# A decode block whose first two weight tensors are stored with wider rows in DRAM

## The chip, the cores and the metric

The kernel runs on one core of one Trainium2 chip. The core has a matrix engine (TensorE, PE in the profile), VectorE (DVE), ScalarE (ACT), GpSimd (POOL) and SyncE (SP), an on-chip memory of 128 partitions (SBUF), accumulators for matrix products (PSUM), and 16 DMA engines that move data between DRAM and SBUF. The metric is the device time of one execution in microseconds (us), as the median of several runs.

## What is computed

A transformer block for one new token of each of 4 sequences, with model width 512: a modulation from the condition `c`, attention of 32 query heads over the last 2048 positions of a cache with 8 key/value heads, and a gated feed-forward part. All tensors are float32.

```python
x = A_x                                            # 4 x 1 x 512
mod = (silu(c) @ w_mod).reshape(4, 6, 1, 512)
sa, ca, ga, sb, cb, gb = (mod[:, n] for n in range(6))
h = layernorm(x) * (1 + ca) + sa
q = (h @ wq), 32 heads of 128
p = softmax(q . k_cache[:, :, 6144:] * 128 ** -0.5)
x = x + ga * ((p . v_cache[:, :, 6144:]) @ wo)
h = layernorm(x) * (1 + cb) + sb
x = x + gb * ((silu(h @ w1) * (h @ w3)) @ w2)
```

## The kernel before, in words

The host (`_layout`, lines 493 to 523) rearranges every tensor so that the kernel can fetch it with few large transfers. Each tensor in DRAM has one row for each of the 128 partitions, and a load (`load`, lines 174 to 178) copies the rows of a tensor, or a range of their columns, to a range of columns of SBUF. Before the change a row is as long as its data, so that the rows of a tensor follow one another without a gap. `w_mod_a` has 4096 elements of the first third of `w_mod` and 32 elements of `x` and `c` in a row: 4128 elements, 16512 B. `wq` has 16144 elements, 64576 B. The other 240 columns of `wq` that would make it 16384 come as `guests`, in eight small loads of three rows each, 5760 B a row (lines 202 to 204).

SBUF holds a ring of three slots of 16384 elements for each partition (lines 162 and 163). `w_mod_a` goes to slot 0 (line 186), `wq` to slot 1 (line 188), and keys and values of group 0 to slot 2 (line 205). A group is one key/value head for all 4 sequences. There are eight groups; the first seven are `kv_in`, each 128 rows of 16384 elements (65536 B). After them come `wo_mod` (half of `wo` and the other two thirds of `w_mod`), `last_k_wo` and `last_v` (keys and values of group 7 and a quarter of `wo`), the rest of `wo`, and `w1`, `w3` and `w2` (lines 393 to 412). `w2` has rows of 28672 B and is fetched in four pieces of columns, 8, 3, 2 and 1 of its 14 blocks (`W2_CUTS`, line 16), that is 16384, 6144, 4096 and 2048 B of each row.

The order of the loads is the order of the program: all of them are issued by SP, except `wq`, which ACT issues on its own queue. SP waits before a load until the slot's former contents were used: the second `kv_in` (line 296) waits for the end of the modulation that reads `w_mod_a`, the third (line 329) for the last query product that reads `wq`, and every later one for the products of an earlier group.

The arithmetic goes as follows. After `w_mod_a` has landed, the condition is activated, `x` is transposed and normalised, and 32 products give shift and scale (`mod_columns`, line 292). Then the queries of all heads are computed from `wq` (lines 306 to 315) and transposed. Each group computes its scores, an exponential, the transposes of the probabilities and the weighted values (`group`, lines 350 to 388). After the last group follow the output projection, the second modulation and the feed-forward part.

A small planner, `Program` (lines 44 to 145), records each operation with the SBUF and PSUM ranges that it touches and adds the waits between engines. All recorded operations carry line 59 in the profile. Ranges in DRAM are not recorded.

Of the kernel before, what the change touches and what calls it, by code (L numbers as in the profile page):

```python
# [9 lines left out]
P = 128  # L10
# [6 lines left out]
GUESTS = 240  # L17
# [130 lines left out]
def block_kernel(nc, w_mod_a, wq, guests, kv_in, wo_mod, last_k_wo, last_v, wo, w1, w3, w2, out):  # L148
# [7 lines left out]
    def sb(name, *shape):  # L156
        return nc.alloc_sbuf_tensor(name, (P, *shape), F32).ap()
# [5 lines left out]
    slots = [ring[:, n * 2 * HALF : (n + 1) * 2 * HALF] for n in range(3)]  # L163
# [10 lines left out]
    def load(dst, src, cuts=(0, 1), queue="sync"):  # L174
        step = src.shape[1] // cuts[-1]
        for lo, hi in zip(cuts[:-1], cuts[1:]):
            do(queue, "dma_start", dst[:, lo * step : hi * step], src[:, lo * step : hi * step])
        return dst[:, : src.shape[1]]
# [4 lines left out]

    first = load(slots[0], w_mod_a)
    wma, xt_sb, ct_sb = first[:, :4096], first[:, 4096:4112], first[:, 4112:]
    wq_t = load(slots[1], wq, queue="scalar")
    do("scalar", "preload_act_table_set", "natural_log_exp_and_others")
    kv = [None] * G  # L190

# [53 lines left out]
    xc, sq, h = (sb(n, P) for n in ("xc", "sq", "h"))  # L245
    ss, ln, r0, ve, a, r = (sb(n, 1) for n in ("ss", "ln", "r0", "ve", "a", "r"))
# [246 lines left out]
def _layout(i):  # L493
    import numpy as np

    def a(t):
        return np.ascontiguousarray(t)

    k = i["A_k_cache"][:, :, SK - W :, :].reshape(B, G, NT, 512, DH)
    v = i["A_v_cache"][:, :, SK - W :, :].reshape(B, G, NT, NC, P, DH)  # L500
    wm = i["w_mod"].reshape(4, P, 6, 4, P)
    xc = np.concatenate([i[n].reshape(B, 4, P).transpose(2, 1, 0).reshape(P, 16) for n in ("A_x", "c")], 1)
    w2 = i["B_w2"].reshape(14, P, D)
    wq = a(i["A_wq"].reshape(4, P, G, 512).transpose(1, 2, 0, 3)).reshape(P, 16384)
    guests = np.zeros((2, 12, 6, GUESTS), np.float32)
    for n, (at, lo, hi) in enumerate(GUEST_AT):
        for m in range(2):
            guests[m, lo:hi, n] = wq[at + 32 * m + lo : at + 32 * m + hi, 16384 - GUESTS :]
    wo = a(i["A_wo"].reshape(2, 4, R, P, D).transpose(0, 3, 1, 2, 4)).reshape(2, P, 8192)
    kv = np.concatenate([k.transpose(1, 4, 2, 0, 3).reshape(G, P, 8192), v.transpose(1, 4, 2, 0, 3, 5).reshape(G, P, 8192)], 2)  # L510
    return {
        "w_mod_a": np.concatenate([a(wm[:, :, :2].transpose(1, 0, 3, 2, 4)).reshape(P, 4096), xc], 1),
        "wq": a(wq[:, : 16384 - GUESTS]),
        "guests": guests.reshape(24, 6 * GUESTS),
        "kv_in": kv[: G - 1],
        "wo_mod": np.concatenate([wo[0], a(wm[:, :, 2:].transpose(1, 0, 3, 2, 4)).reshape(P, 8192)], 1),
        "last_k_wo": np.concatenate([kv[G - 1, :, :8192], wo[1, :, :4096]], 1),
        "last_v": a(kv[G - 1, :, 8192:]),
        "wo": a(wo[1, :, 4096:]),
        "w1": a(i["B_w1"].reshape(4, P, FF).transpose(1, 0, 2)).reshape(P, 4 * FF),  # L520
        "w3": a(i["B_w3"].reshape(4, P, FF).transpose(1, 0, 2)).reshape(P, 4 * FF),
        "w2": a(np.stack([w2[4 * j + c] for c, j in CHUNKS], 1)).reshape(P, NF * D),
    }
# [15 lines left out]
```

## Time and profile before

| | us |
|---|---|
| median of 3 runs | 242.15 |
| lowest and highest | 242.04, 242.48 |
| span of the profiled execution, first to last instruction | 240.8 |
| PE busy | 148.7 (62%) |
| DVE busy | 56.3 (23%) |
| ACT busy | 24.1 (10%) |

The page gives the span of the profiled execution and no time of its own beside it; the median of the runs is 1.35 us longer than the span. The DMA engines read 101.22 MB from DRAM, 420 GB/s over the span. In the tables by slices the span is cut into 40 equal parts, and each digit is a busy share in tenths.

### The profile page before, as it was taken

Reading aid. Unit: us, or ns where it says so; the run is one execution under the profiler, and the core shown is the slowest. Engines: PE = TensorE matmul, PEld = TensorE weight load, DVE = VectorE, ACT = ScalarE, POOL = GpSimd, SP = SyncE. Lnnn points to the kernel's source line nnn. Section 1 sums busy time; section 2 is a strip of 40 time slices with the busy share of each in tenths; the row PEclk is TensorE's granted clock in tenths of the full one; section 3 lists DMA queues with packets and bytes.
Section 4 is the critical chain, followed back from the end, with each engine's and each line's share of the span. In section 5 each row is a group of like instructions: output and inputs, shape, how many; then the busy total and the mean of one; then the engine's idle time right before and its main releaser. Section 6 shows DMA issues by size and latency. Waiting matters only on the chain.

```text
span 240.8 us, 2502 instructions
## 1 busy us (share of the span) xinstructions
PE 148.7 (62%) x1113; PEld 54.2 (22%) x1113; DVE 56.3 (23%) x141; ACT 24.1 (10%) x36; POOL 4.5 (2%) x12
## 2 busy tenths in 40 slices
PE   0000169982984962944867576667399719965876
PEld 0000133322322212201312222221042202422333
DVE  5000231034152024123132133130313104113210
ACT  2000000003003003001100300300200001320100
POOL 7000000000000000000000000000000000000000
PEclk9999997997696798879797799795759968995899
DMA  8999999999999999999999999999999999999994
GB/s 305 434 444 455 424 425 446 416 446 414 457 395 468 403 459 414 449 425 446 425 446 427 435 435 435 435 427 446 425 446 425 411 419 430 386 444 443 401 413 162
DMA packets 2937, 101.39 MB, mean 421 GB/s; under 512 B 472, under 2 KB 472, under 8 KB 880
## 3 DMA queue, kind: packets, MB, share of 16 engines
q1 hardware_dynamic: 2784, 92.99, 89.8%
q10 hardware_dynamic: 144, 8.27, 8.0%
q8 instruction: 8, 0.13, 0.2%
q14 instruction: 1, 0.01, 0.0%
HBM read 101.22 MB, written 0.03 MB: 420 GB/s over the span
## 4 chain that ended last, share of the span: by engine, by line
DMA 60%; PE 31%; DVE 5%; ACT 3%; issue 1%; ACTq 0%
DMA ring<-kv_in 33%; DMA ring<-w 16%; PE s_ps L59 14%; DMA ring<-w_mod_a 11%; PE bank L59 9%; PE o_ps L59 6%; DVE nm L59 3%; ACT p_sb L59 3%; PE a_ps L59 1%; DVE mod_a L59 0%; ACT work L59 0%; DVE p_sb L59 0%; DVE e L59 0%; DVE h L59 0%; DVE sq L59 0%
## 5 line engine op out<-in xcount | busy, mean ns | idle before, releaser
L59 PE MATMUL s_ps<-ring,qT 128*32 128x512 f32 x256 | 36.5, 722 | 20.3 <-DMA ring<-kv_in 13.3
L59 PE MATMUL bank<-ident,p_sb 128*128 128x128 f32 (+1 forms) x136 | 27.7, 353 | 30.8 <-ACT p_sb L59 30.7
L59 PE MATMUL o_ps<-ring,pT 128*16 128x512 f32 x256 | 38.4, 707 | 0.1
L59 PEld LDWEIGHTS bank<-ident,p_sb 128*128 128x128 f32 (+1 forms) x136 | 19.8, 178 | 52.5 <-ACT p_sb L59 31.7
L59 ACT ACTIVATE p_sb<-s_ps,nm 128x2048 f32<-128x2048 f32 (+1 forms) x11 | 16.5, 1501 | 139.7 <-DVE oT L59 104.1
L59 DVE TENSOR_REDUCE nm<-s_ps 128x1 f32<-128x2048 f32 x7 | 16.0, 2292 | 32.5 <-PE s_ps L59 32.5
L59 DVE COPY pT<-bank 128x64 f32<-128x64 f32 x32 | 7.2, 225 | 57.0 <-PE bank L59 57.0
L59 PEld LDWEIGHTS s_ps<-ring,qT 128*32 128x32 f32 x256 | 8.7, 129 | 46.9 <-issue 20.1
L59 PE MATMUL bank<-ident,xs 128*128 128x128 f32 x1 | 0.5, 476 | 27.8 <-POOL xs L59 27.8
L59 PE MATMUL s_ps<-ring,h2T 128*32 128x512 f32 (+1 forms) x64 | 9.0, 657 | 2.3 <-DMA ring<-w 2.3
L59 PE MATMUL s_ps<-ring,hT 128*32 128x512 f32 (+1 forms) x64 | 9.4, 705 | 0.0
L59 PEld LDWEIGHTS o_ps<-ring,pT 128*16 128x16 f32 x256 | 5.4, 99 | 11.9 <-issue 9.0
L59 DVE SCALAR_TENSOR_TENSOR o_own<-o_ps,rl,own 128x512 f32<-128x512 f32 x7 | 5.3, 751 | 11.1 <-PE o_ps L59 11.1
L59 PE MATMUL a_ps<-ring,oT 128*4 128x512 f32 x64 | 7.4, 592 | 0.0
L59 DVE TENSOR_REDUCE o_sum<-o_own 128x128 f32<-128x512 f32 x7 | 7.2, 1034 | 0.2
L59 PE MATMUL bank<-ring,sc 128*32 128x256 f32 (+1 forms) x64 | 6.9, 587 | 0.0
L59 PEld LDWEIGHTS bank<-ident,xs 128*128 128x128 f32 x1 | 0.2, 183 | 27.8 <-POOL xs L59 27.8
L59 DVE TENSOR_SCALAR e<-e 128x16 f32<-128x16 f32 x1 | 0.2, 175 | 23.3 <-ACT e L59 23.3
L59 DVE COPY qT<-bank 128x64 f32<-128x64 f32 x8 | 2.2, 280 | 12.4 <-PE bank L59 12.0
L59 DVE TENSOR_REDUCE mx<-s_ps 128x1 f32<-128x512 f32 x4 | 2.8, 692 | 9.0 <-PE s_ps L59 9.0
L59 PEld LDWEIGHTS s_ps<-ring,h2T 128*32 128x32 f32 x64 | 2.6, 130 | 7.3 <-issue 4.4
L59 PE MATMUL s_ps<-ring,hidT 128*32 128x64 f32 (+1 forms) x112 | 3.6, 274 | 0.3 <-DVE hidT L59 0.3
(97 smaller groups left out, 63.7 us busy)
## 6 DMA issues: line engine op xcount, KB each, us to landing
ring<-wq ACTq DMA_DIRECT2D x1, 8072.0 KB, 26.9
ring<-w SPq DMA_DIRECT2D x2, 3584.0 KB, 37.9
ring<-last_k_wo SPq DMA_DIRECT2D x1, 6144.0 KB, 30.1
ring<-last_v SPq DMA_DIRECT2D x1, 4096.0 KB, 39.5
ring<-w_mod_a SPq DMA_DIRECT2D x1, 2064.0 KB, 26.7
ring<-wo SPq DMA_DIRECT2D x1, 2048.0 KB, 41.8
ring<-w SPq DMA_DIRECT2D x1, 2048.0 KB, 43.1
ring<-w SPq DMA_DIRECT2D x1, 768.0 KB, 44.5
```

The costliest lines, as they stand in the source:

```text
L59: op = Op(engine, lambda: getattr(getattr(self.nc, engine), method)(*args, **kw), [])
```

## The change

The host stores `w_mod_a` with rows of 5120 elements (20480 B) and `wq` with rows of 17408 elements (69632 B). The new function `spaced` puts zeros behind the data of each row. The kernel loads the same columns as before, from the same tensors, in the same order, to the same places. Only the distance from one row to the next in DRAM is another.

```diff
-    first = load(slots[0], w_mod_a)
+    first = load(slots[0], w_mod_a[:, :4128])
     wma, xt_sb, ct_sb = first[:, :4096], first[:, 4096:4112], first[:, 4112:]
-    wq_t = load(slots[1], wq, queue="scalar")
+    wq_t = load(slots[1], wq[:, : 16384 - GUESTS], queue="scalar")
...
+    def spaced(t, row):
+        return np.concatenate([t, np.zeros((P, row - t.shape[1]), np.float32)], 1)
+
...
-        "w_mod_a": np.concatenate([a(wm[:, :, :2].transpose(1, 0, 3, 2, 4)).reshape(P, 4096), xc], 1),
-        "wq": a(wq[:, : 16384 - GUESTS]),
+        "w_mod_a": spaced(np.concatenate([a(wm[:, :, :2].transpose(1, 0, 3, 2, 4)).reshape(P, 4096), xc], 1), 5120),
+        "wq": spaced(wq[:, : 16384 - GUESTS], 17408),
```

## Rows read from the trace of the kernel before

**Rows 1.** The page: span, busy time by engine, and the DMA lines in 40 slices.

```profile
span 240.8 us, 2502 instructions
...
PE 148.7 (62%) x1113; PEld 54.2 (22%) x1113; DVE 56.3 (23%) x141; ACT 24.1 (10%) x36; POOL 4.5 (2%) x12
...
DMA  8999999999999999999999999999999999999994
GB/s 305 434 444 455 424 425 446 416 446 414 457 395 468 403 459 414 449 425 446 425 446 427 435 435 435 435 427 446 425 446 425 411 419 430 386 444 443 401 413 162
```

**Rows 2.** Chain of waits, its load links and the last arithmetic: start, duration (us), what.

```profile
0.73 26.68 DMA ring<-w_mod_a
...
67.41 38.51 DMA ring<-kv_in
...
190.94 38.54 DMA ring<-w
229.48 0.04 issue
229.52 3.71 PE s_ps L59 x20
```

**Rows 3.** Timeline of PE, scores of four groups: start, duration, operation, idle before, releaser.

```profile
86.61 3.64 PE L59 MATMUL s_ps<-ring,qT 128*32 128x512 f32 x32 [2.39 <-DMA ring<-kv_in]
...
105.96 4.93 PE L59 MATMUL s_ps<-ring,qT 128*32 128x512 f32 x32 [3.44 <-DMA ring<-kv_in]
...
125.31 5.34 PE L59 MATMUL s_ps<-ring,qT 128*32 128x512 f32 x32 [2.19 <-DMA ring<-kv_in]
...
144.66 3.64 PE L59 MATMUL s_ps<-ring,qT 128*32 128x512 f32 x32 [1.80 <-DMA ring<-kv_in]
```

**Rows 4.** DMA issues (KB, us to landing), then the timeline of these issues.

```profile
ring<-wq ACTq DMA_DIRECT2D x1, 8072.0 KB, 26.9
ring<-w_mod_a SPq DMA_DIRECT2D x1, 2064.0 KB, 26.7
...
0.73 0.39 ACTq L59 DMA_DIRECT2D ring<-wq  x1
0.73 0.38 SPq L59 DMA_DIRECT2D ring<-w_mod_a  x1
8.95 0.42 SPq L59 DMA_DIRECT2D ring<-kv_in  x1
34.19 14.84 SPq L59 DMA_DIRECT2D ring<-kv_in  x2
```

**Rows 5.** Packets by size, and queues: packets, MB, share of 16 engines.

```profile
DMA packets 2937, 101.39 MB, mean 421 GB/s; under 512 B 472, under 2 KB 472, under 8 KB 880
...
q1 hardware_dynamic: 2784, 92.99, 89.8%
q10 hardware_dynamic: 144, 8.27, 8.0%
```

**Rows 6.** Windows: stretch, busy by engine, PEclk, DMA share, GB/s; two early, three of kv.

```profile
5.90:6.40 0.50, 0.00 (x0) 0.00 (x0) 0.00 (x0) 0.00 (x0) 0.00 (x0) 1.00 4.11 1778
8.90:9.40 0.50, 0.00 (x0) 0.00 (x0) 0.00 (x0) 0.00 (x0) 0.00 (x0) 1.00 4.12 1778
84.30:84.80 0.50, 0.00 (x0) 0.00 (x0) 0.50 (x1) 0.00 (x0) 0.00 (x0) 1.00 2.43 1049
103.70:104.20 0.50, 0.00 (x0) 0.00 (x0) 0.50 (x1) 0.00 (x0) 0.00 (x0) 1.00 2.12 918
144.00:144.50 0.50, 0.00 (x0) 0.00 (x0) 0.50 (x1) 0.00 (x0) 0.00 (x0) 1.00 1.82 786
```

**Rows 7.** Windows of the stretches in which wo, then the first piece of w2 loads.

```profile
208.00:210.00 2.00, 2.00 (x24) 0.59 (x20) 0.08 (x1) 0.00 (x0) 0.00 (x0) 1.00 0.98 418
...
230.00:232.00 2.00, 2.00 (x25) 0.66 (x20) 0.00 (x0) 0.00 (x0) 0.00 (x0) 1.00 0.98 418
```

**Rows 8.** Windows of the first microseconds, and of the rest of the first loads.

```profile
1.00:2.00 1.00, 0.00 (x0) 0.00 (x0) 0.94 (x4) 0.85 (x1) 0.83 (x2) 1.00 0.89 215
2.00:3.00 1.00, 0.00 (x0) 0.00 (x0) 0.97 (x9) 0.43 (x1) 1.00 (x1) 1.00 1.73 631
3.00:4.00 1.00, 0.00 (x0) 0.00 (x0) 0.99 (x9) 0.00 (x0) 1.00 (x4) 1.00 1.07 452
4.00:26.00 22.00, 0.00 (x0) 0.00 (x0) 0.39 (x2) 0.00 (x0) 1.02 (x2) 1.00 0.95 413
```

## The prediction

> **What bounds the kernel now.** I read the page's span and slices first [rows 1]. TensorE is busy 62% of the span, but the DMA line stands at 9 tenths or more in 38 of 40 slices; only the first and the last are lower. The reader is to see one stream of loads, about 101 MB, that never stops. The chain of waits says the same [rows 2]: its long links are loads (w_mod_a, kv_in, w), and after the last w (this is w3) 11.3 us of arithmetic follow, while the pieces of w2 come in. In the timeline of TensorE the scores of one group begin 19.35 us after those of the group before (86.61, 105.96, 125.31, 144.66), each time released by kv_in [rows 3]. One kv load is 128 x 65536 B = 8.389 MB, so it streams at 8.389 MB / 19.35 us = 433.5 GB/s.
>
> The two loads that change open this stream. Both are issued at 0.73 us, on two queues, and land 26.7 and 26.9 us later, side by side; kv_in is issued behind them at 8.95 us and waits in the queue [rows 4]. So the question is only whether the first 27 us of the stream get shorter or longer. If they do, does the end move as well? The next kv load was issued at 34.19 us and the one after it 14.8 us later at most, by 49.0 us [rows 4]. The first loads end at 27.6 us and a kv load takes 19.35 us, so kv[0] ends at about 47 us and kv[1] at about 66 us: each successor is in the queue 13 us or more before its turn. What the first loads win or lose therefore goes through to w3 and the end, one for one.
>
> **The change part by part.** Terms are made against the span of 240.8 us of the profiled execution. The page does not give the time of this execution itself; the median of the three runs is 242.15 us, and I carry the difference of 1.35 us unchanged as what lies around the span.
>
> *Bytes.* The slices in front of the two loads take only the 4128 and 16144 elements that were there before, so the copied bytes stay 2.114 + 8.266 = 10.380 MB. If the unused elements were read too, it would be 128 x (3968 + 5056) B = 1.155 MB more, 2.67 us at 432.6 GB/s; the destination has no place for them, so I take 0.
>
> *Packets.* wq is 144 packets on its queue: 128 of one row each, and 16 more, which I take as one for each of the 16 DMA engines [rows 5]. A source whose rows lie apart could be cut differently. The kernel already has such loads: w2 is fetched in column pieces, with rows of 16384, 6144, 4096 and 2048 B that stand 28672 B apart, and guests by every fourth row. Between 2 KB and 8 KB the page counts 880 - 472 = 408 packets [rows 5], exactly 3 x 128 + 24, one per row. So a row apart from its neighbour is still one packet: 0. Nor is there a new instruction or wait: one issue of 0.38 us on SP and one of 0.39 us on ACT stay [rows 4].
>
> *Steady rate.* In the windows the packets count in the stretch in which they begin, so a short stretch can have a share above 1; GB/s divided by share is the rate while an engine is busy. For wq and w_mod_a it is 1778/4.11 = 432.6 and 1778/4.12 = 431.6 GB/s [rows 6]. For kv, whose rows already start on multiples of 4096 B from each other, it is 431.7, 433.0 and 431.9 [rows 6]. So the odd rows of 16512 and 64576 B run as fast as the aligned ones; there is nothing left to win. The other side is bounded too: wo lies contiguous with rows of 16384 B, the first piece of w2 has the same rows 28672 B apart, an odd multiple of 4096 as in the change, and both show 418 GB/s at a share of 0.98 [rows 7]. So spacing costs nothing either. Bounds from the spread of these quotients: 0.3% of 24 us, 0.07 us to either side; I take 0.
>
> [...]
>
> *The start.* Here the rows do differ. From 1 to 4 us the shares are 0.89, 1.73 and 1.07, while the bytes at 432.6 GB/s would need 215/432.6 = 0.50, 1.46 and 1.04 [rows 8]. The first packets of the sixteen engines are thus slow by 0.39 + 0.27 + 0.03 = 0.69 us each on average, and after that the deficit is gone: 4 to 26 us show 413 GB/s at 0.95 [rows 8]. The first loads last 26.9 us for 10.380 MB / 432.6 = 24.0 us of transfer; 0.7 of the 2.9 us beside it is this. No row shows how much of it hangs on where the rows begin, and there is no second cold start in the trace to compare. Bounds: all of it goes (-0.69 us), or the same again is added (+0.69 us). The nearest row to no effect is the steady stretch, where layout makes no difference, so I take 0 and keep both ends for the range.
>
> *Sum:* 240.8 + 0 + 0 + 0 + 0 = 240.8 us of span, 242.15 us of time. What a measurement of this kernel can tell from no change is about 0.2%, 0.48 us.
>
> **Rivals.** *Forecast, nothing changes, 0.53.* The stream is bound by the engines' own pace and not by where it reads. It gives 242.15, with the spread of the runs shown (242.04 to 242.48).
>
> *The start becomes quicker, 0.27.* For it: the first packets are the only ones below the pace, and they read precisely the two tensors that are moved; 69632 = 17 x 4096 and 20480 = 5 x 4096 place the starts of the sixteen engines' rows differently over the memory. Against it: part of the 0.69 us must be the first access itself, which no layout takes away. All of it gone gives 241.46; the case decides from 0.48 of the 0.69 us on. [...]
>
> *The start becomes slower, 0.18.* Before, consecutive rows begin 128 B and 3136 B further round within 4096 B (16512 = 4 x 4096 + 128, 64576 = 15 x 4096 + 3136); afterwards all begin at the same place in it. If the sixteen first packets, which begin together, then run into each other at the memory, the deficit of 1 to 4 us doubles: 0.69 us more, 242.84. It decides from 0.48 us more. For it: sixteen starts inside about half a microsecond. Against it: kv rows begin in the same way and run at pace [rows 6], though no longer in step.
>
> *The change does something else than it says, 0.02.* The spaced rows are cut or read whole; the price of the second is 2.67 us, 244.8. The packet counts speak against it.
>
> **How the numbers follow.** The likeliest case gives 242.15. Its own range is 241.9 to 242.5: the steady bounds and the spread of the runs. The range over all cases reaches to where the two start rivals would end in full, 241.46 and 242.84: 241.4 to 242.8, leaving out effects beyond the bound and the last rival. Faster 0.27, within 0.2% 0.53, slower 0.18 + 0.02 = 0.20.
>
> **What would show it.** Right: the queue of wq has 144 packets and 8.27 MB; the rate while busy in short stretches before 26 us is 431 to 433 GB/s; the shares of 1 to 4 us still exceed need by 0.6 to 0.8 us; the scores of groups keep 19.35 us between them; w3 arrives within 0.3 us of 229.5. The faster case shows the excess below 0.2 us and w3 at about 228.8; the slower one an excess of about 1.4 us and w3 at about 230.2. The forecast is wrong if the steady quotient moves by a per cent, or if the end moves without the landing of the first loads having moved.

## The result, and the profile after

The changed kernel takes 242.66 us (median of 11 runs, 242.27 to 243.13) where the kernel before takes 242.15 (11 runs, 242.00 to 242.48): a ratio of 1.0018, 95% interval 1.0010 to 1.0026. It is slower by about half a microsecond. That lies inside the stated range, and just inside the 0.2% that the prediction had set as no change; but the interval excludes 1, and the forecast of no effect was wrong.

The page and the DMA view of the kernel after. They answer to [rows 1, 5]: the counts of packets and bytes are the same, the span is 0.5 us longer.

```profile
span 241.3 us, 2502 instructions
...
DMA packets 2937, 101.39 MB, mean 420 GB/s; under 512 B 472, under 2 KB 472, under 8 KB 880
...
q1 hardware_dynamic: 2784, 92.99, 89.6%
q10 hardware_dynamic: 144, 8.27, 7.9%
```

So no row was cut and no unused element read. The two loads themselves land no later than before in this execution, 26.9 and 26.7 us after their issue as in [rows 4]:

```profile
ring<-wq ACTq DMA_DIRECT2D x1, 8072.0 KB, 26.9
...
ring<-w_mod_a SPq DMA_DIRECT2D x1, 2064.0 KB, 26.7
```

The windows of the kernel after (stretch, busy by engine, PEclk, DMA share, GB/s) answer to [rows 6, 8]:

```profile
1.00:2.00 1.00, 0.00 (x0) 0.00 (x0) 0.95 (x4) 0.84 (x1) 0.83 (x2) 1.00 0.89 198
2.00:3.00 1.00, 0.00 (x0) 0.00 (x0) 0.97 (x9) 0.44 (x1) 1.00 (x1) 1.00 1.36 518
3.00:4.00 1.00, 0.00 (x0) 0.00 (x0) 0.99 (x9) 0.00 (x0) 1.00 (x4) 1.00 1.37 581
...
5.90:6.40 0.50, 0.00 (x0) 0.00 (x0) 0.00 (x0) 0.00 (x0) 0.00 (x0) 1.00 3.51 1520
8.90:9.40 0.50, 0.00 (x0) 0.00 (x0) 0.00 (x0) 0.00 (x0) 0.00 (x0) 1.00 3.52 1520
```

The steady rate is 1520/3.51 = 433.0 and 1520/3.52 = 431.8 GB/s, as before. The start is the surprise: shares of 0.89 + 1.36 + 1.37 = 3.62 stand against a need of (198 + 518 + 581)/432.6 = 3.00, an excess of 0.62 us for the mean engine, where it was 0.69 before. A second trace of each kernel (b0 and a4 below) gives 0.74 and 0.68. By the mean engine the start did not become slower, and yet the kernel did.

The timeline of TensorE shows where the time is lost: releases of the scores by a load, to be laid beside [rows 3].

```profile
86.83 5.34 PE L59 MATMUL s_ps<-ring,qT 128*32 128x512 f32 x32 [2.48 <-DMA ring<-kv_in]
106.18 3.64 PE L59 MATMUL s_ps<-ring,qT 128*32 128x512 f32 x32 [1.06 <-DMA ring<-kv_in]
125.53 5.34 PE L59 MATMUL s_ps<-ring,qT 128*32 128x512 f32 x32 [2.99 <-DMA ring<-kv_in]
144.88 3.64 PE L59 MATMUL s_ps<-ring,qT 128*32 128x512 f32 x32 [1.80 <-DMA ring<-kv_in]
...
198.29 6.55 PE L59 MATMUL s_ps<-ring,qT 128*32 128x512 f32 x32 [7.22 <-DMA ring<-last_k_wo]
```

The kv loads keep 19.35 us between them, and each is 0.22 us later than its counterpart (86.61, 105.96, 125.31, 144.66). The last scores are released at 198.29, against 197.90 before. So the lateness comes in two pieces, one before 86 us and one between 145 and 198 us, when wq has long been loaded. From there on this execution follows TensorE: the mean granted clock is 0.56 from 198 to 205 us, where it was 0.80 in the profile before, and the scores take 6.55 us instead of 5.04. The products of w3 begin at 230.18 without a wait for their load, and the end comes 0.5 us later. The clock is not the whole of it: in a second trace of the same kernel (a4) the load of w3 itself is late, and releases them at 230.17 where the kernel before has 229.52.

```profile
86.94 3.64 PE L59 MATMUL s_ps<-ring,qT 128*32 128x512 f32 x32 [0.61 <-DMA ring<-kv_in]
...
198.54 5.85 PE L59 MATMUL s_ps<-ring,qT 128*32 128x512 f32 x32 [7.01 <-DMA ring<-last_k_wo]
...
230.17 3.63 PE L59 MATMUL s_ps<-ring,h2T 128*32 128x512 f32 x32 [0.73 <-DMA ring<-w]
```

The load of w releases these products in seven of the runs below that lose 0.28 us or more (a4, b1, b3, c1, c2, d2, e2).

The first of the two pieces does not by itself tell a slow kernel from a fast one. Run d3 below has both tensors at their old places and takes the time of the kernel before, and its scores are 0.30 us late at 86 us:

```profile
86.91 6.38 PE L59 MATMUL s_ps<-ring,qT 128*32 128x512 f32 x32 [3.54 <-DMA ring<-kv_in]
...
198.18 5.37 PE L59 MATMUL s_ps<-ring,qT 128*32 128x512 f32 x32 [7.02 <-DMA ring<-last_k_wo]
...
229.80 3.63 PE L59 MATMUL s_ps<-ring,h2T 128*32 128x512 f32 x32 [1.35 <-DMA ring<-w]
```

The begin of the products of w3 does tell them apart: 229.52 to 229.81 us in the traces of the kernels that lose at most 0.2 us, 229.96 to 230.57 in all others.

Whose lateness is it? wq's 144 packets are 128 rows and 16 more, which the prediction took as one for each engine. On that reading a load has landed only when the slowest of the sixteen engines has done its part. The windows of the last loads show how many engines are still at work. First the kernel before, in a second trace (the run b0 below):

```profile
237.00:237.50 0.50, 0.50 (x40) 0.37 (x28) 0.00 (x0) 0.50 (x1) 0.00 (x0) 1.00 0.65 250
237.50:238.00 0.50, 0.46 (x35) 0.43 (x34) 0.00 (x0) 0.02 (x1) 0.00 (x0) 1.00 0.09 33
238.00:238.50 0.50, 0.50 (x49) 0.50 (x37) 0.00 (x0) 0.00 (x0) 0.00 (x0) 1.00 0.00 0
```

Then the kernel after:

```profile
237.00:237.50 0.50, 0.50 (x25) 0.24 (x19) 0.00 (x0) 0.00 (x0) 0.00 (x0) 1.00 0.60 234
237.50:238.00 0.50, 0.50 (x44) 0.45 (x33) 0.00 (x0) 0.49 (x1) 0.00 (x0) 1.00 0.21 78
238.00:238.50 0.50, 0.47 (x32) 0.36 (x28) 0.00 (x0) 0.09 (x1) 0.00 (x0) 1.00 0.01 4
```

The reader is to see the tail. At 237 us a third of the engines' time is already unused in both kernels. Before, no packet begins after 238 us; after the change 4 GB/s x 0.5 us = 2 KB do, which is one single row of the last piece of w2. That one late engine is enough to make a load late would fit this; the views do not show the engines one by one. The last column of the table below follows this window through all runs, in one profiled execution of each: where no packet begins after 238 us, no run loses more than 0.2 us; where some do, every run is 0.28 us or more slower.

### The profile page after: what moved, and what is told of

Same layout as the page of the kernel before. It is cut to its first block, busy times and chain, and to the rows that moved or that the text cites. A ratio compares the mean times of both kernels' runs of the same rounds, so it can differ in the third digit from the quotient of the medians.

```text
span 241.3 us, 2502 instructions
## 1 busy us (share of the span) xinstructions
PE 152.2 (63%) x1113; PEld 55.1 (23%) x1113; DVE 56.3 (23%) x141; ACT 24.1 (10%) x36; POOL 4.5 (2%) x12
## 3 DMA queue, kind: packets, MB, share of 16 engines
q10 hardware_dynamic: 144, 8.27, 7.9%
## 4 chain that ended last, share of the span: by engine, by line
DMA 57%; PE 33%; DVE 5%; ACT 4%; issue 1%; ACTq 0%; DVEq 0%
DMA ring<-kv_in 33%; PE s_ps L59 18%; DMA ring<-last_k_wo 13%; DMA ring<-w_mod_a 11%; PE bank L59 8%; PE o_ps L59 6%; ACT p_sb L59 3%; DVE nm L59 2%; ACT work L59 1%; PE a_ps L59 1%; DVE sq L59 0%; DVE h L59 0%; DVE mx L59 0%; DVE mod_a L59 0%; DVE xc L59 0%
## 5 line engine op out<-in xcount | busy, mean ns | idle before, releaser
L59 PE MATMUL s_ps<-ring,qT 128*32 128x512 f32 x256 | 38.3, 753 | 19.1 <-DMA ring<-kv_in 11.8
L59 PE MATMUL bank<-ident,p_sb 128*128 128x128 f32 (+1 forms) x136 | 28.6, 362 | 30.8 <-ACT p_sb L59 30.7
L59 PEld LDWEIGHTS bank<-ident,p_sb 128*128 128x128 f32 (+1 forms) x136 | 20.7, 185 | 52.5 <-ACT p_sb L59 31.7
L59 PE MATMUL bank<-ident,xs 128*128 128x128 f32 x1 | 0.5, 477 | 27.9 <-POOL xs L59 27.9
L59 PE MATMUL s_ps<-ring,h2T 128*32 128x512 f32 (+1 forms) x64 | 10.0, 717 | 0.4 <-DVE h2T L59 0.4
L59 PEld LDWEIGHTS bank<-ident,xs 128*128 128x128 f32 x1 | 0.2, 183 | 27.9 <-POOL xs L59 27.9
L59 PEld LDWEIGHTS s_ps<-ring,hT 128*32 128x32 f32 x64 | 2.4, 125 | 6.0 <-issue 5.9
## 6 DMA issues: line engine op xcount, KB each, us to landing
ring<-wq ACTq DMA_DIRECT2D x1, 8072.0 KB, 26.9
ring<-w_mod_a SPq DMA_DIRECT2D x1, 2064.0 KB, 26.7
```

What stands on the lines that cost most here:

```text
L59: op = Op(engine, lambda: getattr(getattr(self.nc, engine), method)(*args, **kw), [])
```

## The experiments

Every run computes the whole function. The kernel before was timed beside each run, on the same chip; "beside" in the table is its median there. The ratio and its interval are worked out from the single runs (5 to 12 of each version, more of the kernel before), so that they can differ from the quotient of the two medians. The last column is the DMA share and the GB/s in the window from 238.0 to 238.5 us of that run, as in the last row of the two fences above.

| run | what | us | beside | ratio, 95% interval | 238.0 to 238.5 |
|---|---|---|---|---|---|
| a1 | w_mod_a spaced, wq not | 242.73 | 242.17 | 1.0029, 1.0016 to 1.0042 | 0.08, 29 |
| a2 | wq spaced, w_mod_a not | 242.34 | 242.17 | 1.0016, 1.0006 to 1.0027 | 0.00, 0 |
| a3 | sizes of the change, rows contiguous | 242.68 | 242.17 | 1.0027, 1.0014 to 1.0039 | 0.02, 8 |
| a4 | the changed kernel again | 242.65 | 242.17 | 1.0021, 1.0012 to 1.0029 | 0.04, 16 |
| b0 | the kernel before again | 242.19 | 242.19 | 1.0002, 0.9993 to 1.0011 | 0.00, 0 |
| b1 | w_mod_a only longer at its end | 242.80 | 242.19 | 1.0042, 1.0020 to 1.0063 | 0.04, 16 |
| b2 | wq only longer at its end | 242.14 | 242.19 | 0.9998, 0.9989 to 1.0007 | 0.00, 0 |
| b3 | 0.04 MB more in eight small loads | 243.06 | 242.19 | 1.0041, 1.0027 to 1.0055 | 0.12, 45 |
| c1 | wq begins 496 KiB later | 242.94 | 242.15 | 1.0029, 1.0010 to 1.0048 | 0.05, 20 |
| c2 | b1, wq begins 16 KiB later | 242.43 | 242.15 | 1.0010, 0.9993 to 1.0027 | 0.02, 8 |
| c3 | b1, wq begins 528 KiB later | 242.21 | 242.15 | 1.0000, 0.9984 to 1.0015 | 0.00, 0 |
| c4 | b1, wq begins 1552 KiB later | 242.25 | 242.15 | 0.9999, 0.9984 to 1.0014 | 0.00, 0 |
| d1 | the change, wq begins 528 KiB later | 242.25 | 242.16 | 1.0011, 1.0001 to 1.0021 | 0.00, 0 |
| d2 | the change, table load ahead of wq | 242.84 | 242.16 | 1.0036, 1.0023 to 1.0049 | 0.01, 4 |
| d3 | before, table load ahead of wq | 242.19 | 242.16 | 1.0000, 0.9991 to 1.0009 | 0.00, 0 |
| d4 | w_mod_a and wq both 496 KiB later | 242.51 | 242.16 | 1.0015, 1.0006 to 1.0023 | 0.01, 4 |
| e1 | the change, wq issued 2 us later | 243.34 | 242.17 | 1.0055, 1.0036 to 1.0074 | 0.08, 29 |
| e2 | before, wq issued 2 us later | 242.53 | 242.17 | 1.0015, 1.0006 to 1.0024 | 0.07, 25 |

**Is it the rows?** The first theory, S, was that the new row distance makes the start slow. Its rival, A, came from the sizes: more than the distance between the rows is changed. w_mod_a becomes longer by 128 x 3968 B = 507904 B = 496 KiB and wq by 632 KiB, and whatever is stored behind them moves, if the tensors follow one another in DRAM; no view shows their addresses. (The expectations below write 508 KiB for the same 507904 B.) In a1 and a2 one of the two tensors keeps its old form.

> Only w_mod_a has spaced rows (20480 B); wq stays contiguous. Theory S (slow start): the 0.5 us come from the first packets, which are all of w_mod_a and read rows that now begin at the same place within 4096 B; the latest of the sixteen engines then stays late to the end. S expects nearly the whole loss here, +0.3 to +0.5 us against the kernel before. Theory A (addresses): the longer tensors only move every later tensor to other DRAM addresses; w_mod_a grows by 0.5 MB, so A has no reason for a whole loss here and expects +0.0 to +0.3.

> Only wq has spaced rows (69632 B). Theory S: the first packets of w_mod_a are as before; wq's first packets follow behind them, no longer all at once, so -0.2 to +0.2 us. Theory A: wq grows by 0.65 MB, the larger shift, so about +0.2 to +0.4 us.

In a3 both tensors have the new size and the old, contiguous rows:

```diff
-    first = load(slots[0], w_mod_a[:, :4128])
+    first = load(slots[0], w_mod_a.rearrange("p n -> (p n)")[: P * 4128].rearrange("(p n) -> p n", n=4128))
```

(and wq in the same way, with the zeros behind the data of the tensor).

> Both tensors have the size of the changed kernel, but the rows lie contiguous as before and the unused elements stand at the end of each tensor. Theory S: 0 (within 0.15 us) against the kernel before. Theory A: the whole +0.44 us.

> The changed kernel unedited, for a second trace of its first microseconds and a second time. Both theories: +0.3 to +0.6 us against the kernel before. S expects the same engine pattern in the trace: the latest guest load landing about 0.2 us later than before, and kv_in releases about 0.2 us later.

a4 repeats the loss. a3 settles the main point: +0.51 us without any space between rows. S falls; the whole loss is there with the sizes alone, as far as the intervals of a3 and a4 can tell. a1, on which S had staked nearly the whole loss, shows +0.56, but a longer w_mod_a comes with it.

**Which tensor's place?** b1 and b2 lengthen one tensor at its end and leave all rows contiguous.

```diff
-        "wq": a(wq[:, : 16384 - GUESTS]),
+        "wq": longer(wq[:, : 16384 - GUESTS], 17408),
```

(b2; `longer` appends zeros behind the last row. b1 has the same for w_mod_a, to 5120 elements for each partition.)

> The kernel before, unedited, for a second trace. Theory W (the place of wq in DRAM) and theory L (the place of the later tensors) both expect 242.1 to 242.3 us. If the first trace is typical, the last guest load again lands near 28.1 us and the kv scores keep 19.35 us; if the start is a matter of chance in each execution, it lands anywhere up to 28.5.

> w_mod_a keeps its contiguous rows and is longer at its end by the 0.5 MB of the change; wq and all later tensors are untouched but lie 0.5 MB further on, if the tensors follow one another. Theory W: the loss of the run with spaced w_mod_a, +0.4 to +0.6 us, since wq begins at another place. Theory L: only the shift of the later tensors counts, by 0.5 MB instead of the 1.15 MB of the size-only run, so 0 to +0.3. A theory in which the distance between the rows counts expects 0.

> wq keeps its contiguous rows and is longer at its end; it begins where it did, and only the later tensors lie 0.65 MB further on. Theory W: 0 (within 0.15 us). Theory L: the +0.2 to +0.4 us of the run with spaced wq rows, which has the same sizes. If that run is slower than this one, the distance of wq's rows costs the difference.

b1 loses 0.61 us, b2 nothing. So, if the tensors follow one another, moving those behind wq by 632 KiB costs nothing, which speaks against theory L (the place of the later tensors), and moving wq with them by 496 KiB does. That speaks for theory W (the place of wq). The timeline of b1 shows once more that the loss need not appear at the start:

```profile
86.59 3.64 PE L59 MATMUL s_ps<-ring,qT 128*32 128x512 f32 x32 [1.59 <-DMA ring<-kv_in]
...
144.64 5.34 PE L59 MATMUL s_ps<-ring,qT 128*32 128x512 f32 x32 [2.00 <-DMA ring<-kv_in]
...
197.91 6.31 PE L59 MATMUL s_ps<-ring,qT 128*32 128x512 f32 x32 [5.63 <-DMA ring<-last_k_wo]
230.22 3.63 PE L59 MATMUL s_ps<-ring,h2T 128*32 128x512 f32 x32 [0.72 <-DMA ring<-w]
```

Up to 197.91 this kernel is on the times of the kernel before (86.61, 144.66, 197.90), and yet w3 releases its product at 230.22, against 229.52 there. That an engine which was late, but not the latest, got more to do after 198 us would fit, and is not seen. What the late work was, no view names. The page counts eight packets of 16 KB on a queue of kind instruction in this run and in both profiles, beside the loads that the kernel issues; that they are the late work is only argued.

**Does one late engine set the end?** b3 adds eight loads of three rows to the kernel before:

```diff
+    for m in range(2):
+        for c in range(4):
+            do("sync", "dma_start", p_all[32 * m + c : 32 * m + 12 : 4, 1632:], kv_in[0][32 * m + c : 32 * m + 12 : 4, :416])
```

> The kernel before with eight more loads of three rows of 1664 B each behind the guests, into unused columns: 0.04 MB, 0.09 us of the sixteen engines' common rate, but by the trace's rate of 27 GB/s for one engine 8 x 62 ns = 0.5 us on the three engines that carry three-row loads (plus some 10 ns for each load's end). The theory that the latest single engine sets the end expects +0.4 to +0.6 us; the theory that the mean over the engines counts expects +0.0 to +0.1 us.

It is +0.87 us for 40 KB, more than the 0.5 that one engine's share explains by the estimate above, and far from the 0.1 of the mean. The page counts 48 packets more on the queue, 24 rows and 24 others, three for each load where wq has sixteen; that agrees with three engines for each load. So does the trace of the kernel before, in windows of 0.02 us: from 27.2 to 27.9 us the guests begin three rows every 0.22 us, and one row of 5760 B takes a share of 0.69, 0.69 x 16 x 0.02 = 0.22 us of one engine or 26 GB/s. A window without data (26.42 to 26.44 us, 0 GB/s) has a share of 0.03, or 0.03 x 16 x 0.02 = 0.01 us of one engine, which fits the 10 ns that the expectation adds for a load's end. The queue of b3:

```profile
q1 hardware_dynamic: 2832, 93.03, 89.6%
```

Its tail:

```profile
237.00:237.50 0.50, 0.50 (x16) 0.20 (x11) 0.00 (x0) 0.00 (x0) 0.00 (x0) 1.00 0.57 225
237.50:238.00 0.50, 0.50 (x47) 0.50 (x43) 0.00 (x0) 0.33 (x1) 0.00 (x0) 1.00 0.26 98
238.00:238.50 0.50, 0.46 (x32) 0.30 (x25) 0.00 (x0) 0.26 (x1) 0.00 (x0) 1.00 0.12 45
```

At 238 to 238.5 us 0.12 x 16 = two engines' worth of time is busy. The scores of group 2 are released at 87.45 where b0 has 86.66, so the added work delays the whole chain at once. That it does so because few engines carry it is not separated from a fixed price of about 0.1 us for each of the eight loads: no run spreads the same 40 KB over all sixteen.

**Can the place be given back?** In c1 w_mod_a is untouched and wq begins 496 KiB inside a longer tensor. In c2 to c4 w_mod_a is longer as in b1, and wq begins 16, 528 or 1552 KiB inside its tensor; its distance from the begin of w_mod_a then equals the old one modulo 512 KiB, 1 MiB and 2 MiB. Counted from the begin of w_mod_a, and if the tensors follow one another, wq begins at 2064 KiB in the kernel before, at 2560 in the changed one, in b1 and in c1, at 2576 in c2, at 3088 in c3 and at 4112 in c4.

```diff
-    wq_t = load(slots[1], wq, queue="scalar")
+    wq_t = load(slots[1], wq.rearrange("p n -> (p n)")[126976 : 126976 + P * (16384 - GUESTS)].rearrange("(p n) -> p n", n=16384 - GUESTS), queue="scalar")
```

(c1; 126976 elements are 496 KiB.)

> w_mod_a as before. wq contiguous, but its data begin 508 KiB inside a tensor that is 1.6 MB longer; 508 KiB is what the change adds to w_mod_a ahead of wq. Theory W (the place at which wq is read decides): the loss of the changed kernel, +0.4 to +0.6 us. Theory M (the length of w_mod_a's own tensor or the place of the later tensors decides): 0, within 0.15 us.

> w_mod_a contiguous and longer at its end by 508 KiB, as in the run with the longer w_mod_a; wq contiguous, beginning 16 KiB inside its longer tensor, so that the distance from the begin of w_mod_a to that of wq is again 16 KiB beyond a multiple of 512 KiB, as before. Theory W with a period of 512 KiB or less: 0 (within 0.2 us). Theory W with a longer period, and theory M: +0.4 to +0.6 us.

> The same with wq beginning 528 KiB inside its tensor: the distance is 16 KiB beyond a multiple of 1 MiB, as before. Theory W with a period of 1 MiB or less: 0 (within 0.2 us); with a period of 2 MiB, and theory M: +0.4 to +0.6 us.

> The same with wq beginning 1552 KiB inside its tensor: the distance is 16 KiB beyond a multiple of 2 MiB, as before. Theory W with a period of 2 MiB or less: 0 (within 0.2 us). Theory M: +0.4 to +0.6 us in all three of these runs.

c1 has the loss with w_mod_a untouched, so the half of theory M by which w_mod_a's own length decides falls. c3 and c4 bring the time of the kernel before back with w_mod_a as long as in the change. c2 stands between, and its interval holds both answers. The other half of M, the place of the later tensors, is not tested cleanly: the longer wq tensor moves them by 1600 KiB in c1 and by 2096 in c2 to c4. A place of the later tensors that is bad when they move by 496, 1128 or 1600 KiB and good at 632, 2096 or 2664 would fit too. The place at which wq is read fits with less: every run with wq 496 KiB further on loses 0.35 us or more, and every run with wq where it was or whole MiB further on 0.17 us or less (leaving out b3, which adds loads, and e2, which issues wq later). A period is not shown: whole steps of 1 MiB are good twice, one place is bad, and c2 leaves open whether 512 KiB would do.

d1 does the same with the changed kernel itself, both row distances kept:

> The changed kernel with both row distances, but wq beginning 528 KiB inside a longer tensor, so that its distance from w_mod_a is 16 KiB beyond a multiple of 1 MiB, as before. If only the place counts: the time of the kernel before, within 0.2 us. If the row distance costs something of its own (the run with wq alone spaced was 0.17 us slower, the one with wq merely longer was not): +0.15 to +0.3 us. If the row distance makes the loss: +0.5 us.

+0.09 us in the median, and an interval of 1.0001 to 1.0021: by the median most of the loss is gone with the spaced rows still there. Seven of its eleven runs lie below 242.3 us, against one of 22 of the changed kernel (the result and a4). What is left for the spacing lies between 0 and 0.5 us by that interval. a2 and b2, which have the same sizes and differ in the rows of wq alone, say about 0.2 (+0.17 and -0.05 us against the runs beside them). So the row distance may cost a little of its own; it gains nothing.

**Why does the place count?** Theory X: the two loads run into each other at the start. Theory P: the place counts by itself.

> w_mod_a contiguous and beginning 508 KiB inside its longer tensor; wq, behind it, is thereby 508 KiB further on too, and the distance between the two is that of before. Theory X: no loss, within 0.15 us. Theory P: +0.4 to +0.6 us.

> The changed kernel with the ACT table load issued ahead of wq instead of behind it, so that wq is issued about 1.3 us later. Theory X (the first packets of the two loads run into each other): the loss goes, 242.1 to 242.3 us, as in the next run. Theory P (wq's place by itself decides): it stays, 242.5 to 242.8 us. The engines have w_mod_a packets in the meantime, so the later issue by itself costs under 0.1 us by either.

> The kernel before with the same later issue of wq. Both theories: 242.1 to 242.3 us, 0 within 0.15 us against the kernel before. If the start had slack to give, this run would be faster by up to 0.3 us.

d4 moves both tensors together and loses 0.35 us, between the two: the distance between the tensors alone does not decide, and neither theory has this size. d2 and d3 did not do what they were made for: the trace of d2 shows the table load and wq's issue next to each other,

```profile
0.73 1.28 ACT L59 ACT_TABLE_LOAD   x1 [0.73 <-PEq L535]
...
0.76 0.38 ACTq L59 DMA_DIRECT2D ring<-wq  x1
```

so that wq is issued 0.03 us later and not 1.3. They only repeat that the new place loses (+0.68) and the old does not (+0.03). e1 and e2 make ACT wait:

```diff
+    do("vector", "memset", slots[1][:, :2048], 0.0)
     wq_t = load(slots[1], wq[:, : 16384 - GUESTS], queue="scalar")
```

> The changed kernel with a VectorE memset of 2048 columns of wq's slot ahead of the load, so that ACT issues wq some 2 us later (about 2.8 instead of 0.73 us) and the first packets of w_mod_a have the memory to themselves; the engines have 5 us of w_mod_a packets, so nothing idles. Theory X (the two loads run into each other at the start): the loss goes, 242.1 to 242.3 us and equal to the next run within 0.15. Theory P (the places alone decide): 242.5 to 242.9 us, 0.4 to 0.6 more than the next run.

> The kernel before with the same wait ahead of wq. Theory P: as before, 242.1 to 242.3 us. Theory X: as before or up to 0.3 us faster, as the start has less to run into. A theory that the start of the engines is simply disturbed by any later second load expects it slower by 0.2 us or more.

wq is now issued at 3.03 us in both. The loss at the new place is still there, 243.34 against 242.53, and larger; X, in which the first packets of wq and w_mod_a disturb each other, falls. That the two loads disturb each other later, while both still run, is not excluded. The later issue also changes the order of the stream, since w_mod_a then lands 12 to 13 us after its issue and the next loads mix with wq, so that the two runs are compared with each other only. The windows of e2 add one thing:

```profile
1.00:2.00 1.00, 0.00 (x0) 0.00 (x0) 0.77 (x1) 0.00 (x0) 0.82 (x2) 1.00 1.25 215
2.00:3.00 1.00, 0.00 (x0) 0.00 (x0) 1.00 (x2) 0.00 (x0) 1.00 (x1) 1.00 0.43 99
...
4.00:5.00 1.00, 0.00 (x0) 0.00 (x0) 0.96 (x11) 0.71 (x1) 0.91 (x2) 1.00 1.00 429
```

Up to 3 us w_mod_a is the only load under way, and its first packets need 1.25 + 0.43 = 1.68 where (215 + 99)/432.6 = 0.73 would do. The slow start is there without wq.

What stays open is why the place of wq decides how late the stream becomes. That in c1 the engines read it 496 KiB further on in its tensor is sure; that the memory serves some sets of addresses less evenly would fit, and no run here separates it from other reasons. No engine can be named in these views, so that a late engine, and its meeting with later work, is concluded from the times and the tails, not seen.

## Why the prediction was right or wrong

*What bounds the kernel* held in the main: the stream of loads, and lateness in it going on to w3 (230.17 in a4). The kv loads of the kernel after are 0.22 us late, each by the same amount, 19.35 us apart. In the profiled execution TensorE sets the end from 198 us on, which the prediction did not foresee. And its question, "only whether the first 27 us of the stream get shorter or longer", was too narrow: the two loads land after 26.7 and 26.9 us as before, while the scores are 0.22 us late at 86 us and 0.39 us at 198 (in a4 the loads land 0.2 us later, and w3 is 0.65 us late). The prediction had named this as a sign that it would be wrong, an end that moves "without the landing of the first loads having moved".

*Bytes, packets and steady rate* held, each at the numbers named: 144 packets and 8.27 MB on wq's queue, 432 to 433 GB/s while busy. One reading was too wide: the two early windows of [rows 6] price wq and not w_mod_a, since their 889 KB are 13 rows of wq and 3 of w_mod_a. Rows of w_mod_a alone show 429 GB/s at a share of 1.00 (e2, 4 to 5 us), within about 1% of it. The aligned rows show no better quotient, 433.0 and 431.8 GB/s against 432.6 and 431.6 before, and d1, which has them with wq at a good place, is not faster (+0.09 us).

*The start* is the step that failed, "I take 0 and keep both ends for the range", in three ways. It looked only at where the rows begin within their tensor, and missed that a longer w_mod_a moves wq by 496 KiB, if the tensors follow one another; b1 and c1 show a loss of 0.61 and 0.79 us with wq so moved and all rows contiguous, a3 one of 0.51 with all the sizes of the change, and in c3, c4 and d1 it is down to 0.06 to 0.10 us. It priced the start by the mean of the sixteen engines: that mean went from 0.69 to 0.62 us while the kernel became slower. That the latest engine counts instead is argued from b3, where 40 KB cost 0.87 us, and not seen. And it took the lateness of a start as fixed from then on, while in b1 no scores are more than 0.1 us late up to 198 us and w3 is 0.7 us late after that. What in the memory makes the place count stays open.

*The rival of a slower start* had the sign and nearly the size (0.69 us against 0.51 measured), but for a reason that fell: row starts at the same place within 4096 B cost at most a part of it. Its sign at the start, a doubled excess from 1 to 4 us, did not appear; its other sign, w3 at about 230.2, did (230.18, and 230.17 in a4), from another cause. The sixteen starts that it put inside half a microsecond take about one: in the trace of the kernel before thirteen packets begin between 1.5 and 2 us (429 GB/s, 214.5 KB), three more by 2.5 (99 GB/s, 49.5 KB). The rival of a quicker start and the one of cut rows had nothing for them. How much of the start's 0.69 us is the first access itself, the argument set against a quicker start, no run shows; the excess was 0.69, 0.74 and 0.70 us with the old rows (before, b0, d3) and 0.62, 0.68 and 0.55 with the new (after, a4, d2).

*The numbers.* 242.66 lies in the range of 241.4 to 242.8, which the bound for the start had kept open; that is luck, since the doubling from which the bound comes did not happen. The ratio of 1.0018 is just short of the 0.2% from which it would count as slower; the likeliest case's own range, 241.9 to 242.5, misses it. The 0.18 for a slower start was too little.

## What to carry to other kernels

In this kernel, whose loads keep the DMA engines at 9 tenths or more in 38 of 40 slices, 40 KB in small transfers cost 0.87 us where the mean share of sixteen engines says 0.09 (b3). So a change to the start or to small transfers is not to be priced by a mean share; the latest engine's schedule (estimated at 0.5 us here) comes nearer, and still falls short. A change in a tensor's length can cost time with every row as it was (b1, +0.61 us for a w_mod_a that is only longer at its end): before a gain or a loss of some tenths of a per cent is put down to a new layout, run the new sizes with the old layout. And a load that lands on time (26.7 and 26.9 us here) says little about the loads behind it: look at the last ones. Here no version beat the kernel before; the old layout and sizes stay.

## What the runs showed of the hardware that was not expected

The place of one tensor in DRAM moved the whole kernel by 0.5 to 0.8 us of 242 (c1 against c3, 242.94 and 242.21), at an unchanged busy rate (432.6 GB/s from 5.9 to 6.4 us before the change and 433.0 after it, 433 and 434 in c1 and c3). The first packets of the stream are slow even while one load runs alone: 1.68 against 0.73 us of engine time in e2. Forty KB in eight loads of three rows cost 0.87 us, as much as 0.38 MB spread evenly would at 432.6 GB/s. And a DMA issue that stands behind an ACT table load in ScalarE's program did not wait for its 1.28 us: it came 0.03 us after the load began.
